# Cosine attention and a highway layer on one Trainium2 core: v's loads on GpSimd's queue, quadrant scores, more turning on TensorE, a new order

## The chip, the cores and the metric

The kernel runs on one core of a Trainium2 chip (trn2). The metric is the time of one execution on the device in microseconds (us). A core has five engines with queues of their own: TensorE (PE: matmuls, and PEld for its weight loads), VectorE (DVE), ScalarE (ACT), GpSimd (POOL) and SyncE (SP). Each works through its instructions in the order in which the program lists them. SP and POOL also issue the transfers (DMAs) here, which 16 DMA engines carry out.

## The reference

```python
def _attn_ref(q, k, v, tau):                   # 8 batches, 12 heads, 448 rows, 64 columns, fp32
    q_n = q / (np.linalg.norm(q, axis=-1, keepdims=True) + 1e-06)
    k_n = k / (np.linalg.norm(k, axis=-1, keepdims=True) + 1e-06)
    scores = np.matmul(q_n, k_n.transpose(0, 1, 3, 2)) / tau
    scores = scores - np.max(scores, axis=-1, keepdims=True)
    attn = np.exp(scores)
    attn = attn / (np.sum(attn, axis=-1, keepdims=True) + 1e-09)
    return np.matmul(attn, v).astype(np.float32)

def _moe_ref(x, w_h, w_t, b_t):                # x: 3584 tokens, 768 columns
    H = np.maximum(x @ w_h, 0.0)
    T = 1.0 / (1.0 + np.exp(-(x @ w_t + b_t)))
    return (T * H + (1.0 - T) * x).astype(np.float32)
```

`reference` runs the attention, puts the heads of a token side by side (`x` is batch and row by head and column), and runs the highway layer on that.

## The kernel before

**Tiling.** Two heads, one of each half of the twelve, form a pair; there are 48 pairs, six to a batch. The 448 rows of a head lie as three columns of 128 partitions and a rest of 64 rows, and the rests of two heads share a column. A finished batch gives three tiles of 128 tokens for the highway layer (`xb`), and the rests of two batches give one more (`xl`): 28 tiles.

**A pair, step by step.** For each batch, q and k are loaded into `raw` (L477, L480 and, for the rests, L494) and turned from fp32 into fp16 on the way. VectorE squares them (`sq`, L532; ScalarE may do it in batch 0, L530), adds up in three steps (L539, L546, L551) and takes the inverse root by a polynomial of six small instructions (L560 to L565, `rs`). A pair's q and k are then scaled into `qkn` (L589, two instructions, on GpSimd, or on VectorE for the first twelve pairs) and turned into `qkT`. For the first six pairs TensorE turns them (L602, seven matmuls with the identity `ident`) and ScalarE or VectorE copies the result out of PSUM (L611, L613); for the others it is a DMA transpose that SP issues (L618). Then come the scores in four steps `qk..._0` to `qk..._3`. Steps 0 to 2 are two matmuls each, in two row halves of the array with 128 columns (L656); step 3 is two matmuls in two 64x64 quadrants (L658). ScalarE takes the exponential of each step (L672, L674). `av` multiplies by v and by a column of ones (L695, 32 matmuls), and `un` divides by the sum (L703, L705, L709).

**v.** A batch of v comes into `vraw` (fp32, L503, 1152 KB, issued by SP) and is cast into `vp` by ScalarE or VectorE (`vc`, L633 or L635); the rests of v go straight into `vp` (`x`, L510, issued by GpSimd).

**The highway layer.** A tile of `xb` is turned by a DMA transpose that SP issues (L747) into `xT`. Four groups `ff` follow (two weights by two halves): six matmuls each (L760), and a seventh for the bias with `w_t` (L763). VectorE takes `d` (L771), ScalarE the tanh (L779), and VectorE ends every second tile in four instructions on PSUM (`e` and `o`, L793, L799), the others in `g` (L809), `h` (L814) and a sum on GpSimd or VectorE (`o`, L822). SP stores (`st`, L836, L839).

**The order.** No loop sets the order. Every piece of work is an `Op` with engines that may do it and their costs, what it depends on, the buffers it takes and gives back (`Ring`), and a step. `Planner.plan` runs a clock over these costs and each time gives a free engine the ready op with the lowest step; it holds DMA queues as `Queues`, in which two transfers side by side pay `MIX`. The steps come from the list `RANKS`, one number for each op. Loads of later batches also wait for the first score step of a pair, and which pair it is stands in the list `HOLDS` (`gates`). What the plan gives is the fixed order of each engine's queue. `NPE = 6` says how many pairs TensorE turns.

Of the kernel before, what the change touches and what calls it, by code (L numbers as in the profile page):

```python
# [20 lines left out]
    -4726, -5034, -3968, -6443, -5016, -1052, -269, -2602, -2552, -2596, -434, 2262, -9024, -8900, -8904, -8800, -8800, -8800,  # L21
    -7024, -8476, -5024, -5024, -4900, -5336, -2524, -2524, -2400, -2398, -2300, -2300, -2300, -2300, 2560, 2976, 3100, 3100,
    3200, 3200, 3200, 3200, 8681, 8922, 9100, 9100, 9200, 9200, 9200, 9200, 14976, 14976, 15100, 15100, 16488, 14761, 15200,
    15200, 20976, 19572, 21100, 21100, 20761, 20761, 21200, 21079, 28179, 28033, 26810, 27100, 25473, 27597, 28022, 27647, 33521,
    33521, 33100, 32877, 33597, 33597, 36754, 33124, -3725, -5674, -5574, 664, 326, 521, 8327, 6326, 6426, 14275, 12373, 11899,
    20275, 20754, 20440, 26230, 25378, 25478, 30637, 32457, 31478, 38275, 36326, 35718, -4873, -5000, -5521, -3528, -4000, -4000,
    -4521, -2528, -2000, -2000, -2521, 2513, -4653, -3653, -1653, 1000, 1000, 1000, 2472, 4000, 3346, 4835, 5472, 1347, 4347,
    6147, 6066, 8213, 8472, 9562, 11213, 11213, 11472, 7347, 13986, 12988, 12500, 14411, 16000, 15546, 12862, 17472, 13347, 17921,
    19000, 19642, 20472, 20589, 22261, 22642, 23472, 18217, 27536, 24941, 24941, 26626, 30536, 27941, 28000, 29472, 25446, 31000,
    31000, 33461, 33230, 34000, 34000, 36173, 35472, 31347, 36112, 36911, 38291, 38472, 40000, 40871, 40000, 38094, 37278, -3500,  # L30
    -3874, -2735, 3134, -2500, -2500, -5046, -40, -1500, -1500, -735, 555, -500, -1324, -799, 499, 500, 500, 1949, -664, 1500,
    3454, 6101, 3555, 2500, 2500, 5167, 3500, 3500, 3645, 3309, 4287, 5258, 5500, 6285, 7156, 7091, 3248, 7258, 7530, 7530, 8529,
    8530, 8500, 10860, 9500, 9079, 11410, 9209, 9209, 12299, 10177, 6379, 13652, 11209, 11209, 15313, 12209, 12209, 16506, 13209,
    13209, 17101, 14209, 14209, 20025, 15209, 15209, 18354, 21987, 17500, 19354, 18500, 18500, 19500, 19500, 18257, 20500, 20500,
    20500, 21500, 21500, 21500, 22500, 22500, 22234, 18725, 23500, 23500, 24204, 26263, 26263, 25534, 27263, 27263, 26500, 28263,
    28263, 27500, 28907, 29263, 28500, 30263, 30263, 31742, 31263, 31263, 30500, 32263, 31630, 31402, 31429, 31500, 32500, 32394,
    32662, 33500, 31201, 33500, 34672, 35218, 34500, 35329, 35486, 35486, 36500, 36818, 36818, 35559, 37500, 37380, 38443, 38380,
    38380, 39500, 38956, 39734, 40500, 40592, 40592, 45215, 41500, 42120, 42322, 42500, 42500, 43322, 44100, 43500, 44322, -675,
    -1000, 5940, 5940, 4026, 9101, 11990, 8050, 9260, 9260, 11841, 15131, 17188, 19871, 20000, 20000, 23000, 24559, 26000, 25079,
    28962, 28451, 32000, 32000, 35000, 35000, 38811, 38811, 41779, 41811, 44000, 44000, 0, 255, 483, 255, 0, 255, 320, 255, 780,  # L40
    900, -1531, 1255, 1000, 1255, 727, 1255, 1000, 1255, 1800, 1891, 696, 2255, 1952, 2255, 2000, 2255, 2000, 2255, 2097, 3767,
    3000, 3136, 3000, 7706, 3000, 2030, 3000, 3136, 3659, 4767, 4000, 3726, 4000, 4255, 4000, 6338, 4000, 4255, 4001, 5767, 4445,
    5255, 5000, 3824, 5000, -3485, 5000, 5255, 5800, 6805, 6000, 7308, 6000, 6255, 6000, 6255, 5623, 6188, 6800, 7272, 7000, 7255,
    7000, 7255, 7000, 7255, 7000, 7255, 7800, 8557, 8000, 8255, 8000, 8230, 8000, 8255, 8000, 8255, 9063, 9767, 9000, 8318, 9000,
    8318, 7689, 8318, 8696, 8318, 9066, 10767, 10000, 12149, 8424, 12808, 10000, 12149, 10000, 12149, 11336, 12489, 11000, 11255,
    10957, 12031, 11000, 11255, 11000, 11255, 11800, 13138, 11857, 12255, 12000, 11895, 12000, 12255, 12000, 12255, 12800, 13767,
    13000, 13255, 13098, 13255, 13000, 14172, 13208, 13255, 16128, 14283, 14000, 14666, 14000, 14255, 14000, 14255, 14715, 14255,
    14800, 14907, 15846, 12782, 15000, 12905, 15622, 12782, 15000, 12782, 15370, 15659, 15208, 15348, 16000, 16255, 16000, 16255,
    16000, 16255, 16800, 17695, 17000, 17805, 17000, 17255, 17000, 17255, 16652, 17255, 17800, 18695, 18000, 18255, 17947, 17991,
    18000, 18255, 18000, 18255, 18800, 19695, 20515, 19255, 20515, 19255, 20515, 19255, 18122, 19255, 20058, 20695, 20000, 20065,  # L50
    20000, 20255, 20000, 20255, 20000, 20255, 19820, 20117, 21083, 21255, 21083, 21255, 21989, 21255, 21393, 21255, 21800, 22695,
    22054, 22255, 21859, 22255, 22237, 23729, 22083, 23465, 22800, 18604, 23083, 24465, 22185, 24465, 23083, 24419, 23078, 24836,
    23822, 27342, 24083, 25318, 24083, 25360, 25764, 25465, 24083, 25465, 24970, 24900, 24921, 26403, 25083, 26468, 25073, 25143,
    24840, 25255, 25800, 26779, 26083, 25996, 24842, 29084, 26083, 25996, 26083, 25996, 26855, 26900, 27083, 26371, 27083, 27017,
    27083, 27017, 27083, 27017, 27800, 27640, 28083, 28224, 28083, 28224, 28083, 28224, 28083, 28224, 27293, 28900, 29083, 29255,
    28137, 29255, 29083, 29255, 28445, 29719, 26915, 29900, 30313, 30255, 30083, 30255, 30000, 30255, 29946, 30428, 27715, 30900,
    31000, 31103, 30423, 31255, 31000, 30253, 31000, 31255, 31567, 31900, 32000, 31568, 32000, 28459, 32000, 28459, 32000, 28459,
    34051, 32900, 31338, 32865, 33000, 33255, 33000, 31864, 33624, 33199, 33567, 33900, 34000, 34255, 34000, 28710, 34000, 28566,
    34668, 28257, 34668, 34900, 35000, 29566, 34843, 29566, 35000, 29566, 35000, 30566, 34777, 35900, 35990, 36255, 36000, 36255,
    36000, 36255, 35741, 33192, 36338, 36900, 37000, 36694, 37000, 37255, 37000, 37255, 37000, 37255, 37567, 37900, 38000, 38475,  # L60
    38241, 38505, 38000, 38475, 38000, 38475, 36529, 39084, 39000, 39255, 39000, 39255, 39000, 40759, 31104, 38789, 40104, 39900,
    40000, 40095, 40000, 40255, 40000, 40255, 40000, 40255, 40567, 43475, 41000, 41255, 41000, 41255, 39907, 41255, 41000, 41255,
    41567, 41900, 42000, 42255, 42000, 42255, 42000, 42255, 42000, 42255, 42800, 42900, 43000, 43255, 41657, 43255, 43000, 43255,
    43000, 43587, 43800, 43900, 44772, 44255, 44261, 44255, 44000, 44456, 44000, 44255, 43771, 45094, 45000, 40783, 44549, 40783,
    45000, 40534, 45000, 40783, 45800, 40862, 46000, 60154, 46000, 45825, 46000, 46472, 44492, 46255, 46800, 39268, 47000, 47108,
    47000, 47255, 47000, 47255, 47000, 47255, 47800, 46158, 3336, 12000, 16736, 23769, 30000, 36634, 42236, 49318, 7317, 9872,
    6036, 9961, 6174, 13150, 319, 8481, 319, 7800, 7800, 7900, 8000, 9317, 11661, 7874, 11914, 8174, 12043, 1692, 12561, 1822,
    4825, 8778, 3458, 8778, 10000, 11317, 13661, 9874, 13961, 9798, 14261, 6557, 14561, 4319, 11800, 6292, 11900, 12000, 13317,
    15661, 9487, 15961, 10483, 16261, 6319, 16561, 6319, 13818, 12577, 13477, 12800, 14000, 14846, 17805, 13474, 17561, 13774,
    17861, 8264, 18161, 7919, 15533, 15147, 15140, 15600, 16390, 18861, 15074, 19161, 15374, 19461, 9519, 19761, 10220, 16817,  # L70
    16689, 16817, 16689, 17200, 14751, 20332, 16674, 20942, 16974, 21783, 12265, 21361, 15417, 18600, 18286, 18700, 18528, 18136,
    16739, 17874, 21961, 18174, 22261, 15472, 22561, 15472, 18352, 18800, 17392, 18800, 19849, 20136, 23661, 19850, 24131, 19737,
# [38 lines left out]
class Ring:  # L111


    def __init__(self, bufs):
        self.free = list(range(len(bufs)))
        self.bufs = bufs
        self.where = {}

    def __getitem__(self, key):
        return self.bufs[self.where[key]]  # L120


class Queues:

# [220 lines left out]
def swdge():  # L345
    return {"POOL": (800, 800, 0.0, False)}
# [558 lines left out]
```

## Time and profile before

| | |
|---|---|
| three runs | 308.23, 304.39, 301.03 us; median 304.39 |
| the profiled execution | 306.19 us, of which the span in the profile is 304.4 us; mean granted clock of TensorE 0.961 |
| PE busy | 245.1 us (81%), 2690 matmuls |
| DVE busy | 226.5 us (74%) |
| ACT busy | 186.3 us (61%) |
| POOL busy | 144.9 us (48%) |
| DMA | q1 (SP's) 57.5%, q0 (POOL's) 44.3% of 16 engines' span |

"Busy" is the time in which at least one instruction of the engine was running. Matmuls overlap each other and their ends are modelled, so the step from one start to the next says more than their length. The span runs from the first to the last instruction; the execution's own time is 1.8 us more.

### The profile page before, as it was taken

The numbers are of one execution on the slowest core, as the hardware profiler recorded it, in microseconds if no ns is written. First come the engines' busy times: TensorE is split into PE (matmuls) and PEld (weight loads), VectorE is DVE, ScalarE is ACT, GpSimd is POOL, SyncE is SP. The second block draws the span as 40 slices with busy tenths as digits, with TensorE's granted clock in tenths as the row PEclk, the third lists the DMA queues.
The fourth block names the chain that finished last, engine by engine and source line by source line (L and its number), as shares of the span: only waits on it lengthen the run. The fifth ranks groups of instructions, "written<-read, shape, count | busy, mean of one in ns | idle before, by whom it ended". The sixth has DMA issues, their size and how long they took to land.

```text
span 304.4 us, 6908 instructions
## 1 busy us (share of the span) xinstructions
PE 245.1 (81%) x2690; PEld 143.0 (47%) x2690; DVE 226.5 (74%) x471; ACT 186.3 (61%) x277; POOL 144.9 (48%) x182
## 2 busy tenths in 40 slices
PE   0032884499498689997999969999699998999992
PEld 0012543155254446553655646465345565556661
DVE  2339689986569976998669896998969865545563
ACT  0273897378557277686659766885178998661221
POOL 8881452036636289337935575547550491002202
PEclk9999999599989999999999998999989999999997
DMA  8999998899969899999999998999999199324523
GB/s 179 118 193 198 177 241 85 145 146 228 141 117 221 137 277 156 213 168 240 228 209 182 178 146 197 135 263 235 187 216 173 65 156 142 71 53 120 155 106 103
DMA packets 125156, 50.99 MB, mean 168 GB/s; under 512 B 106690, under 2 KB 121538, under 8 KB 125123
## 3 DMA queue, kind: packets, MB, share of 16 engines
q1 hardware_dynamic: 79170, 36.39, 57.5%
q0 software_dynamic: 45952, 14.16, 44.3%
q8 instruction: 21, 0.34, 0.4%
q14 instruction: 13, 0.10, 0.1%
HBM read 37.75 MB, written 11.01 MB: 160 GB/s over the span
## 4 chain that ended last, share of the span: by engine, by line
PE 52%; DVE 19%; DMA 15%; ACT 5%; issue 5%; POOL 1%; SPq 1%; DVEq 0%; ACTq 0%; POOLq 0%
PE pb L760 29%; PE pb L695 11%; PE sc L656 7%; DMA vraw<-in_v_dram 7%; ACT ex L672 3%; PE sl L658 3%; DMA w_h<-in_moe_w_h_dram 2%; DMA raw<-in_k_dram 2%; PE pb L763 2%; DMA qkT<-qkn 2%; DVE xb L705 2%; DVE t L809 1%; DVE n L551 1%; DVE sq L532 1%; DVE qkn L589 1%
## 5 line engine op out<-in xcount | busy, mean ns | idle before, releaser
L672 ACT ACTIVATE ex<-sc 128x896 f16<-128x896 f32 x144 | 125.9, 929 | 29.4 <-PE sc L656 29.2
L760 PEld LDWEIGHTS <-xT 128*128 128x128 f16 x672 | 61.8, 99 | 63.3 <-issue 28.9
L589 POOL TENSOR_TENSOR qkn<-raw,rs 128x448 f16<-128x448 f16 x74 | 70.0, 976 | 34.0 <-issue 18.9
L760 PE MATMUL pb<-w_t,xT 128*128 128x384 f16 x336 | 67.3, 339 | 7.5 <-DVE o L799 4.4
L760 PE MATMUL pb<-w_h,xT 128*128 128x384 f16 x336 | 63.8, 331 | 3.2 <-DVE o L799 3.2
L695 PE MATMUL pb<-vp,ex 128*128 128x65 f16 x1536 | 58.4, 195 | 5.9 <-ACT vp L633 3.1
L695 PEld LDWEIGHTS <-ex 128*128 128x128 f16 x1536 | 55.2, 99 | 15.5 <-issue 11.4
L656 PE MATMUL sc<-qkT 64*128 64x448 f16 x288 | 47.0, 370 | 15.3 <-DMA qkT<-qkn 7.2
L771 DVE SCALAR_TENSOR_TENSOR d<-pb,xb 128x384 f16<-128x384 f32 x48 | 26.5, 553 | 11.5 <-PE pb L760 11.1
L779 ACT ACTIVATE pb<-pb 128x384 f32<-128x384 f32 x28 | 13.5, 484 | 28.6 <-PE pb L763 28.3
L779 ACT ACTIVATE t<-pb 128x384 f16<-128x384 f32 x28 | 14.0, 502 | 26.2 <-PE pb L763 26.2
L656 PEld LDWEIGHTS <-qkT 64*128 64x128 f16 x288 | 11.9, 95 | 36.7 <-issue 24.3
L532 DVE TENSOR_TENSOR sq<-raw 128x2688 f16<-128x2688 f16 x15 | 25.2, 1689 | 4.4 <-DMA raw<-in_q_dram 2.4
L705 DVE TENSOR_TENSOR xb<-pb,rd 128x384 f16<-128x384 f32 x48 | 26.8, 558 | 1.7
L822 POOL TENSOR_TENSOR o<-d,xb 128x768 f32<-128x768 f16 x4 | 6.6, 1639 | 45.0 <-DVE d L814 45.0
L510 POOL DMA_DIRECT2D vp<-in_v_dram x16 | 10.9, 682 | 34.5 <-PE sc L656 33.3
L674 ACT ACTIVATE ex<-sl 128x448 f16<-128x448 f32 x48 | 26.9, 561 | 0.4 <-PE sl L658 0.3
L793 DVE SCALAR_TENSOR_TENSOR pb<-pb,d 128x384 f32<-128x384 f32 x28 | 15.6, 562 | 11.6 <-ACT pb L779 11.4
L602 PE MATMUL pb<-ident,qkn 128*128 128x128 f16 x42 | 4.9, 290 | 21.4 <-DVE qkn L589 21.2
L539 DVE TENSOR_TENSOR f<-sq 128x1344 f16<-128x1344 f16 (+2 forms) x17 | 13.8, 810 | 11.0 <-ACT sq L530 10.9
L480 POOL DMA_DIRECT2D raw<-in_k_dram x16 | 13.3, 837 | 14.6 <-PE sc L656 14.4
L763 PE MATMUL pb<-brow,ones 128*128 128x384 f16 x56 | 18.9, 337 | 0.0
(53 smaller groups left out, 239.8 us busy)
## 6 DMA issues: line engine op xcount, KB each, us to landing
vraw<-in_v_dram SPq DMA_DIRECT2D x8, 1152.0 KB, 8.0
out_dram<-o SPq DMA_DIRECT2D x24, 384.0 KB, 2.7
raw<-in_k_dram POOLq DMA_DIRECT2D x14, 288.0 KB, 8.1
raw<-in_q_dram POOLq DMA_DIRECT2D x14, 288.0 KB, 9.0
out_dram<-o SPq DMA_DIRECT2D x8, 192.0 KB, 3.0
w_h<-in_moe_w_h_dram POOLq DMA_DIRECT2D x2, 576.0 KB, 7.1
w_t<-in_moe_w_t_dram POOLq DMA_DIRECT2D x2, 576.0 KB, 10.2
raw<-in_k_dram POOLq DMA_DIRECT2D x16, 48.0 KB, 7.2
```

Source lines behind the costliest of these rows:

```text
L532: nc.vector.tensor_mul(o, r, r)
L589: eng.tensor_mul(qkn_r[n][:, :, g, :], raw_r[b][:, 42 * g + 7 * hn : 42 * g + 7 * hn + 7], rs_r[b][:, g, h].unsqueeze(2).to_broadcast([128 ...
L656: last = nc.tensor.matmul(sc_r[n, j][:, g, 0:S], lhsT=T[:, 128 * j : 128 * j + 128], rhs=rhs, start=True, stop=True)
L672: nc.scalar.activation(o, sc_r[n, j][:, :, 0:S], AF.Exp, scale=inv_tau / (NSC * NSC))
L674: nc.scalar.activation(ex[:, 3136 : 3136 + S], sl_r[n][:, 0:S], AF.Exp, scale=inv_tau / (NSC * NSC))
L695: nc.tensor.matmul(u[:, s * 65 : s * 65 + 65], lhsT=l, rhs=r, start=(m == 0), stop=(m == len(ms) - 1))
L705: nc.vector.tensor_tensor(out=xo, in0=u[:, 0:6, 0:D].rearrange("p (g i) e -> p g i e", g=2), in1=rd[:, 0:6].rearrange("p (g i) -> p g i", ...
L760: nc.tensor.matmul(pt[:, 0:MH], lhsT=xT[:, c, :], rhs=w_sb[w][:, c, ms], start=(c == 0), stop=(w == 0 and c == CC - 1))
L763: nc.tensor.matmul(pt[:, 0:MH], lhsT=ones[:, :], rhs=brow[:, ms], start=False, stop=True)
L771: nc.vector.scalar_tensor_tensor(out=d_r[m][:, h], in0=pb_r[m, w, h][:, 0:MH], scalar=0.0, in1=xsrc()[:, ms], op0=ALU.max, op1=ALU.subtract)
L779: nc.scalar.activation(src if flat else t_r[m][:, h], src, AF.Tanh, scale=0.5)
L793: nc.vector.scalar_tensor_tensor(out=t, in0=t, scalar=1.0, in1=d_r[m][:, h], op0=ALU.add, op1=ALU.mult)
```

## The change

v's loads are issued by GpSimd in place of SP, and the order that `vl[0]` had behind the first load of `raw` is dropped. The score steps 0 to 2 become four matmuls of 64 columns in the four 64x64 quadrants in place of two of 128 columns; step 3 stays as it was. TensorE turns the first twelve pairs (`TPE`, six before) and the first three tiles of x (`XPE`, none before; the copy out of PSUM is done by ScalarE or VectorE). ScalarE may do the squares of batches 0 and 1 (batch 0 before). A first exponential on a small tile (`warm`) stands at the head of ScalarE's queue. Buffers are given back after the last of all their users (`users`), in place of after one named op. Some costs in the planner differ, and `RANKS` and `HOLDS` are new numbers throughout, so the order on every engine is new.

```diff
-    MIX = 12
+    MIX = 4
...
+            for ring, key in op.drops:
+                ring.users[key] = ring.users.get(key, 0) + 1
...
             for ring, key in op.drops:
-                pend.append((op.end + self.SYNC, ring, ring.where[key]))
+                ring.users[key] -= 1
+                if ring.users[key] == 0:
+                    pend.append((op.end + self.SYNC, ring, ring.where[key]))
...
 def swdge():
-    return {"POOL": (800, 800, 0.0, False)}
+    return {"POOL": (730, 730, 0.0, False)}
...
+    def init_act(op):
+        nc.vector.memset(warm[:, :], 0.0)
+        nc.scalar.activation(warm[:, :], warm[:, :], AF.Exp)
+
+    add("warm", {"ACT": (1500, 1500, 0.0, False)}, -30, init_act)
...
         def v_fn(op, b=b):
-            return nc.sync.dma_start(vraw_r[b][:, :, :, :].rearrange("p h c d -> p h (c d)"), heads[2][b])
+            return nc.gpsimd.dma_start(vraw_r[b][:, :, :, :].rearrange("p h c d -> p h (c d)"), heads[2][b])
 
-        vl[b] = add(f"v{b}", sp(650), 6 * b - 4, v_fn, takes=[(vraw_r, b)], dma=("load", 96, 36, 1300, 600))
+        vl[b] = add(f"v{b}", swdge(), 6 * b - 4, v_fn, takes=[(vraw_r, b)], dma=("load", 96, 36, 2200, 800))
...
-            sq = add(f"sq{b}_{lo}", {**dve(n * 64, 2, True), **(act(n * 64) if b == 0 else {})}, s0, sq_fn, deps=ld[b, lo] + ld[b, hi - 1], takes=[(sq_r, key)])
+            sq = add(f"sq{b}_{lo}", {**dve(n * 64, 2, True), **(act(n * 64) if b < 2 else {})}, s0, sq_fn, deps=ld[b, lo] + ld[b, hi - 1], takes=[(sq_r, key)])
...
-    NPE = 6
+    TPE = set(range(12))
...
-        if n < NPE:
+        if n in TPE:
...
                     if j < 3:
-                        last = nc.tensor.matmul(sc_r[n, j][:, g, 0:S], lhsT=T[:, 128 * j : 128 * j + 128], rhs=rhs, start=True, stop=True)
+                        for i in range(2):
+                            o = slice(64 * i, 64 * i + 64)
+                            last = nc.tensor.matmul(sc_r[n, j][o, g, 0:S], lhsT=T[:, 128 * j + 64 * i : 128 * j + 64 * i + 64],
+                                                    rhs=rhs, start=True, stop=True)
...
+        if m in XPE:
+            def xp_fn(op, m=m, xsrc=xsrc):
+                ps = pb_r["x", m][:, 0 : 64 * CC].bitcast(FP16)
+                for c in range(CC):
+                    nc.tensor.transpose(ps[:, 128 * c : 128 * c + 128], xsrc()[:, 128 * c : 128 * c + 128], ident[:, :])
...
-    vl[0].after.append(ld[0, 0][-1])
```

What the new lists make of the head of three queues (the number behind a name is that of the batch for `l`, `r`, `x`, `v`, `sq` and `vc`, and of the pair for the rest; `l` loads q or k, `r` their rests, `x` the rests of v, `w` a quarter of the weights, `iex` clears an `ex` buffer, `nm` is the scaling, `cp` the copy of a turned pair):

```
POOL before: l0 r0 l0 r0 r0 r0 l0 l0 iex x0 x0 l0 iex l0 l0 l0 w ident w iex w l1 l1 l1 l1 r1 r1 nm5 r1 r1 w x1 l2 x1
POOL after:  l0 r0 l0 ident r0 r0 r0 l0 iex l0 l0 l0 l0 l0 iex v0 iex x0 x0 l1 l1 l1 nm1 l1 r1 r1 r1 r1 w w nm3 w nm4 v1 x1
ACT before:  sq0 cp0 ex0 ex0 ex0 ex0 sq0 vc0 vc0 vc0 vc0 cp1 cp2 ex1 ex1 cp4
ACT after:   warm sq0 cp0 sq0 ex0 ex0 ex0 vc0 vc0 ex0 vc0 vc0 cp1 ex1 ex1 ex1 ex1 cp5 sq1 cp3 ex2
SP before:   bias v0 v1 sh0 tr6 tr7 xt0 tr8 tr9 tr10 xt1 tr11 xt2 v2 tr12
SP after:    bias sh0 tr12 st1 tr13 xt3 tr14
```

(`tr` and `xt` are the DMA transposes of a pair and of a tile, `sh` the moves of the rests' output, `st` the stores.) On GpSimd's queue v2 stands behind six of batch 3's eight loads and in front of the scaling of pair 12. On TensorE the order of pairs is no longer one after the other everywhere: pair 29 comes before 26, 40 before 37, 46 before 42.

## The prediction

> **What bounds the kernel now.** I read the page's busy times and chain first, then a table of busy times by stage, then the timeline, and from the starts of the matmuls in it the gaps of TensorE.
>
> ```profile
> PE 245.1 (81%) x2690; PEld 143.0 (47%) x2690; DVE 226.5 (74%) x471; ACT 186.3 (61%) x277; POOL 144.9 (48%) x182
> ...
> PE 52%; DVE 19%; DMA 15%; ACT 5%; issue 5%; POOL 1%; SPq 1%; DVEq 0%; ACTq 0%; POOLq 0%
> ```
> ```profile
> 0.00:15.90 15.90, 0.02 (x1) 0.02 (x2) 5.48 (x23) 2.23 (x2) 13.83 (x30) 1.00 1.09 150
> 15.90:57.30 41.40, 22.02 (x286) 14.04 (x287) 32.63 (x77) 27.06 (x38) 17.15 (x25) 0.94 1.23 175
> 57.30:66.30 9.00, 8.31 (x94) 4.16 (x93) 8.01 (x13) 6.85 (x9) 2.21 (x4) 0.73 0.96 157
> 66.30:110.00 43.70, 34.78 (x383) 19.39 (x382) 34.20 (x70) 25.90 (x39) 22.54 (x26) 0.96 1.12 171
> 110.00:170.00 60.00, 57.51 (x642) 33.22 (x640) 48.72 (x98) 44.10 (x68) 38.08 (x46) 1.00 1.26 210
> 170.00:225.00 55.00, 49.79 (x545) 29.16 (x542) 47.08 (x85) 33.89 (x53) 31.03 (x37) 0.94 1.22 191
> 225.00:298.50 73.50, 72.63 (x756) 42.98 (x754) 48.81 (x108) 45.89 (x72) 20.11 (x19) 1.00 0.56 117
> ```
>
> The columns are stage, length, then PE, PEld, DVE, ACT and POOL busy. TensorE is the bound once it runs; it starts at 15.9 us, limps to 57, and is not full from 66 to 110 and from 170 to 225. I took each gap between two matmul starts, less the pitch of that shape where nothing waits (198 ns for 448 columns, 162 for 384, 31 for 65) and less 95 ns where the array's mode changes. What is over 0.15 us sums to 48.0 us: 22.0 to 57.3 us, 2.5 to 66.3, 11.3 to 110, 2.8 to 170, 8.4 to 225, 1.0 after. So 304.4 = 15.9 start + 234.5 work + 48.0 stalls + 6.0 tail. What stands behind the stalls:
>
> ```profile
> 1.25 6.84 DMA raw<-in_k_dram
> ...
> 65.92 13.72 DMA vraw<-in_v_dram
> 79.66 1.41 DVE vp L635 x2
> ```
> ```profile
> q1 hardware_dynamic: 1554, 1.18, 54.4%
> q0 software_dynamic: 1002, 0.25, 31.4%
> ```
> ```profile
> 175.47 5.50 DVE L814 TENSOR_TENSOR d<-t,d 128x768 f16<-128x768 f16 x1
> 175.93 0.55 ACT L674 ACTIVATE ex<-sl 128x448 f16<-128x448 f32 x1
> 176.05 4.51 POOL L589 TENSOR_TENSOR qkn<-raw,rs 128x448 f16<-128x448 f16 x5
> ```
>
> The first is from the chain of waits: the first k takes 6.8 us to land, and v2 13.7 us, while VectorE stands before its cast. The second is the DMA view of the first 8 us (packets, MB, share): SP's queue has moved all of v0 (1.18 MB) while q and k, issued at the same time, have 0.25 MB. The third is the timeline: `h`, median 0.56 us, takes 5.5 while GpSimd scales pairs back to back. TensorE then stands for PSUM that VectorE has to free (3.1 us at 179; at 215 the same with `g`, 4.2).
>
> **What the Trainium skill says.** "DMA: Bandwidth & Descriptors", Issuing engines are not separate DMA queues: transfers of all engines interleave on the same 16 DMA engines. The trace agrees only in part: beside v0 GpSimd's queue hardly moved. "SBUF — State Buffer", Who interferes with whom: a VectorE instruction with two SBUF inputs blocks against a GpSimd one that reads SBUF. The `h` above agrees. "TensorEngine Tiling (Array Packing)", Key Properties and Restrictions: changing the tiling mode drains the array, and column tiling turns fast weight load off. The trace agrees on the first (a change adds 81 to 108 ns to the pitch); for the second, a quadrant's weight load takes 103 ns against 93. "TensorE: Matmul & The Clock Gate", Step-by-step: weights are pulled ahead of running matmuls. For 64x128 the trace has that (the second step's weights 12 ns after the first step's matmul began); quadrant steps never follow one another in it.
>
> **The change part by part, against the profiled execution's span.**
>
> *Start.* v0 no longer runs beside q and k. The sixth load, the last that the first square needs, was issued at 5.0 and landed at 9.9; `ident` (0.65 us) now stands ahead of it, so 5.65. Loads of the same size (`vp`, L510) land after 2.7 us at best, 3.9 in the median; I take 3.2: 8.9. The table load (1.28 us, shown below) now lies under that wait. The square starts at 8.9 in place of 11.27, and the first turning, 4.6 us on, at 13.5 in place of 15.9.
>
> ```profile
> 9.97 1.28 ACT L530 ACT_TABLE_LOAD   x1 [9.97 <-DMA raw<-in_q_dram]
> ...
> 21.23 1.72 ACT L530 ACTIVATE sq<-raw 128x1792 f16<-128x1792 f16 x1
> ```
>
> *Second pair.* ScalarE ends `cp0` at 15.4, then squares the large part (128x2688: 1.72 x 1.5, an estimate of 2.6) to 18.0, three `ex` at 0.93, one at 0.56 and two `vc` at 0.68 before `ex0_3` to 22.7. v0 is issued near 12.5 behind fewer bytes and lands near 18.5, in time. `av0` (1.0), and `pt1` at about 23.5. VectorE's part for pair 1 (square 1.1, sums 1.6, inverse root 1.3, scaling 0.6) ends near 21, hidden. Before, `pt1` started at 30.8.
>
> *ScalarE's ramp.* Until the first batch is done TensorE has no highway work and ScalarE sets the pace. From `cp1` at 24.4 to the end of `ex7`: seven pairs at 3.35 (3 x 0.93 + 0.56), three `cp` at 0.91, a square 2.6, three `vc` 2.1: 30.8, and 1 for gaps: 56.2. In the old order `ex7` ended near 65. It had a hole of 6.6 us of TensorE from 50 to 56.6, where pair 6 waited for VectorE and for the first DMA transposes (2.9 to 11.6 us, median 3.6); pairs 6 to 11 have none now. Their 42 turnings and the tiles' 18, at up to 107 ns, are 6.4 us of TensorE inside this ScalarE-bound stage; without that cover they would cost it. Copies: 4 more on VectorE, 2 on ScalarE, in the sum. From 57.5 TensorE runs on. At 66 it has ended `qk10_2`, `av7` and all four groups of tile 0; before, at 67.1, `qk8_3`, `av7` and two groups. The lead is 1.1 + seven score steps (1.4) + two groups (2.3) + changes 0.3: 5.1 us.
>
> *After 66 us: v.* Of 23.5 us stalls, 5.9 are v2's (78 to 85), 5.4 VectorE's backlog behind it (to 110), 2.0 v4's (landed 10.3 us after issue), 0.5 v6's: 13.8. On GpSimd's queue a v has its own turn: about 3.2 us of moving (1.18 MB at the 370 GB/s or so of that DMA view's best slices) and 3.2 of latency, 6.5 with no backlog. v2 is issued behind `qk9_0`; its first cast is some 10 us of TensorE work later. v7 is tightest, 8 us. I keep 3 of 13.8. GpSimd pays eight issues at 0.84 to 1.2 us and eight more scalings at 0.94: 16 us more of 145 busy, beside other work.
>
> *Blocked VectorE.* 82 scalings on GpSimd, 74 before; both orders have long runs of them. VectorE loses eight scalings, two squares and six casts and gains five copies: 9 us less. I keep these 7.3 us, and 2.4 of small ones. New: x6 takes `vp` only after `av35`, and `av36` follows 5 us later against 0.7 + 3.9: 1.0. Stalls after 66: 13.7, that is 9.8 less.
>
> *Mode changes.* Counted in the order of TensorE: 217 before, 172 after; after the point above 181 and 141. Before 181 x 0.095 = 17.2; after, into quadrants 94 and out of them 108 ns, 141 x 0.101 = 14.3: 2.9 less.
>
> *Quadrants.* All four share the stream of 448 columns, so no gain; +0 if weights are pulled ahead, +0.1 us a step if not. I take 4 ns for 117 later steps: 0.5.
>
> Sum: 304.4 - 5.1 - 9.8 - 2.9 + 0.5 = 287.1 us of span, 288.9 as an execution. The profiled one was 306.19 against a median of 304.39; in that measure 287.2, rounded to 287.5.
>
> **Rivals.** (a) The later stalls stay (VectorE held by GpSimd, loads late elsewhere): 287.1 + 9.8 = 297 span, 297 as a median, 2.4% faster. For: the fixed orders bet on durations, and transposes vary from 2.9 to 11.6 us. Against: v's lateness is named in the chain. (b) Quadrant weights are not pulled ahead: 117 x 0.1 = 11.7, 299, within 2%. (c) Better: the v stalls go entirely, VectorE's relief takes half of the blocked time, and 13.7 falls to 6: 279.5. (d) Slower: GpSimd's queue sets the pace at each batch turn. Pair 12's scaling stands behind v2 and two loads that wait for `qk11_0`: 0.68 + 0.84 + 1.87, then a transpose of 3.6, 7.0 us, against 8.8 of TensorE work up to `qk12_0`: 1.8 slack. If v's packets lengthen that by 6.3, six turns lose 4.5 each: 27, 314. It passes before's time at 2.8 us a turn and +2% at 3.8.
>
> **How the numbers follow.** Forecast 0.50, (a) 0.20, (b) 0.08, (c) 0.13, (d) 0.09. A change of about 2% is what a measurement of this kernel can tell from none. Faster: 0.50 + 0.13 + 0.14 of (a) = 0.77; same: 0.06 of (a) and (b) 0.08 = 0.14; slower 0.09. Range 275 to 302: (c) less 4.5 and (b) with 3 on top, which is the doubt about the lead at 66 us; (d) is outside.
>
> **What would show it.** Right: first turning at 13 to 14 us, `pt1` before 25, no PE hole at 50 to 57, v landing in 6 to 8 us with no cast waiting over 1 us, 448-column steps 200 ns apart. Wrong: steps 300 ns apart; GpSimd's loads waiting while `qk` waits for `qkT`; VectorE's `g`, `h` and squares stretched by more than 20 us in sum.

## The result, and the profile after

The changed kernel takes 316.64 us (median of four runs, 316.22 to 317.75), the kernel before, run beside it, 302.85: ratio 1.048 [1.040, 1.057] (the brackets are a 95% interval). It is slower. A ratio, here and below, compares the undisturbed executions of the two kernels alone, so it need not be the quotient of their medians. The profiled span is 314.5 us, at a granted clock of 0.962 against 0.961.

From the page, busy times and chain of the changed kernel:

```profile
PE 251.8 (80%) x3038; PEld 150.0 (48%) x3038; DVE 222.2 (71%) x460; ACT 196.8 (63%) x289; POOL 165.6 (53%) x200
...
PE 44%; DMA 18%; DVE 16%; POOL 10%; issue 5%; ACT 3%; SPq 2%; DVEq 0%; POOLq 0%; ACTq 0%
PE pb L804 26%; DMA qkT<-qkn 9%; PE pb L720 8%; DMA xT<-xb 6%; PE sc L680 6%; POOL qkn L609 5%; DVE sq L551 3%; DMA raw<-in_q_dram 2%; DVE qkn L609 2%; PE pb L807 2%; POOL raw L513 2%; POOL raw L499 2%; DVE f L558 1%; DVE n L570 1%; DVE o L866 1%
```

GpSimd has grown by 21 us and VectorE has shrunk by 4, but what is new is the second line's POOL, and what its DMA is made of. v's load is in the chain no longer; in its place stand the two kinds of DMA transposes (`qkT<-qkn`, `xT<-xb`). The table by stage (length, then PE, PEld, DVE, ACT, POOL busy, granted clock, DMA share, GB/s) shows where:

```profile
12.90:57.30 44.40, 30.30 (x427) 20.20 (x428) 35.22 (x77) 35.90 (x46) 28.75 (x38) 1.00 1.14 172
57.30:66.30 9.00, 8.81 (x110) 5.26 (x110) 7.34 (x12) 8.74 (x13) 6.39 (x10) 1.00 1.64 178
66.30:110.00 43.70, 36.24 (x456) 20.85 (x451) 32.55 (x69) 28.45 (x44) 22.71 (x28) 0.92 1.06 167
110.00:170.00 60.00, 48.23 (x596) 28.04 (x594) 38.19 (x78) 37.62 (x56) 38.96 (x43) 0.94 1.14 185
170.00:225.00 55.00, 47.07 (x524) 27.12 (x524) 41.94 (x77) 29.84 (x45) 27.65 (x32) 0.94 0.95 148
```

Up to 66.3 us TensorE does more than before (it starts at 12.9). From 110 to 170 us it now idles 11.8 us, against 2.5. Stalls counted as in the prediction: 40.0 us after 66.3 us, against 23.5 before and 13.7 forecast. Put into the prediction's sum, 287.1 + 26.3 = 313.4, that is nearly all of the miss. (Of the 40.0, 29 are in the view of waits and some 5 are steps at half speed after long stands, for which see the last section.) What TensorE waited for most after 66 us, changed kernel first, then the kernel before (line that waits <- releaser: us in all, times, longest):

```profile
PE sc L680 <- DMA qkT<-qkn: 12.9, 6, 5.7
PE pb L804 <- DMA xT<-xb: 7.1, 3, 5.0
PE pb L804 <- DVE d L815: 2.5, 1, 2.5
PE sc L680 <- ACT ex L697: 2.0, 6, 0.5
PE pb L720 <- DVE o L843: 1.9, 1, 1.9
```
```profile
PE pb L760 <- DVE o L799: 7.6, 4, 4.4
PE sc L656 <- ACT ex L672: 3.6, 3, 1.9
PE pb L760 <- DVE d L771: 2.1, 1, 2.1
...
PE sc L656 <- DMA qkT<-qkn: 0.7, 2, 0.6
```

Before, TensorE waited for VectorE. After, it waits 20.0 us for transposes, in nine waits. The longest, from the timeline and the chain of the changed kernel (start, length, what):

```profile
73.87 1.07 POOL L522 DMA_DIRECT2D vraw<-in_v_dram  x1
```
```profile
73.94 9.56 DMA qkT<-qkn
```
```profile
75.65 2.20 PE L720 MATMUL pb<-vp,ex 128*128 128x65 f16 x64
83.55 0.96 PE L680 MATMUL sc<-qkT 64*64 64x448 f16 x8 [5.69 <-DMA qkT<-qkn]
```

v3 and pair 12's transpose are issued in the same 0.1 us, from two queues. The transpose lands after 9.6 us and TensorE stands for it. The DMA view from 76 to 80 us (packets, MB, share) says what the DMA engines did meanwhile:

```profile
q0 software_dynamic: 188, 0.87, 78.2%
q1 hardware_dynamic: 462, 0.12, 20.0%
```

GpSimd's queue moves 0.87 MB, SP's 0.12. The same view from 75 to 77.1 us, and then from 77.1 to 79.5, shows that it isn't a slow trickle:

```profile
q1 hardware_dynamic: 896, 0.23, 83.5%
q0 software_dynamic: 15, 0.07, 9.0%
```
```profile
q0 software_dynamic: 145, 0.67, 100.6%
```

By 77.1 us the transpose's whole 0.23 MB (128x896 in fp16) has moved. After that SP's queue moves nothing for 2.4 us, though a store and a second transpose have been issued on it. A transfer has landed when its semaphore has had sixteen updates; those of the transpose come in the trace between 80.6 and 83.5 us, each about 0.2 us ahead of one of v3's. So it ends when v3 ends, 6.4 us after its last data packet began. Why its end stands behind v3, the trace doesn't tell. The first 8 us of the kernel before are the same with the roles exchanged: v0 on SP's queue moved first, and GpSimd's queue moved nothing until 5.5 us, though its first load was issued at 1.25. It is not always so: where both queues move, they go packet for packet (631 against 628 in the kernel before from 74 to 77 us), and the longer packets take the more bytes.

Over the 54 transposes with a landing in the trace: with nothing of GpSimd's queue in flight at their issue the median is 2.8 us (24 of them, the longest 5.5), with 400 KB or more, of v or of q and k, it is 8.5 us (18 of them, from 2.7 to 10.3).

### The profile page after: what moved, and what is told of

Same layout as the page of the kernel before. It is cut to its first block, busy times and chain, and to the rows that moved or that the text cites. A ratio compares the mean times of both kernels' runs of the same rounds, so it can differ in the third digit from the quotient of the medians.

```text
span 314.5 us, 7570 instructions
## 1 busy us (share of the span) xinstructions
PE 251.8 (80%) x3038; PEld 150.0 (48%) x3038; DVE 222.2 (71%) x460; ACT 196.8 (63%) x289; POOL 165.6 (53%) x200
## 4 chain that ended last, share of the span: by engine, by line
PE 44%; DMA 18%; DVE 16%; POOL 10%; issue 5%; ACT 3%; SPq 2%; DVEq 0%; POOLq 0%; ACTq 0%
PE pb L804 26%; DMA qkT<-qkn 9%; PE pb L720 8%; DMA xT<-xb 6%; PE sc L680 6%; POOL qkn L609 5%; DVE sq L551 3%; DMA raw<-in_q_dram 2%; DVE qkn L609 2%; PE pb L807 2%; POOL raw L513 2%; POOL raw L499 2%; DVE f L558 1%; DVE n L570 1%; DVE o L866 1%
## 5 line engine op out<-in xcount | busy, mean ns | idle before, releaser
L804 PEld LDWEIGHTS <-xT 128*128 128x128 f16 x672 | 63.2, 100 | 67.5 <-issue 25.4
L609 POOL TENSOR_TENSOR qkn<-raw,rs 128x448 f16<-128x448 f16 x82 | 79.3, 990 | 20.4 <-DVE rs L584 13.2
L680 PE MATMUL sc<-qkT 64*64 64x448 f16 x576 | 52.9, 392 | 25.9 <-DMA qkT<-qkn 12.9
L804 PE MATMUL pb<-w_h,xT 128*128 128x384 f16 x336 | 65.3, 339 | 8.4 <-DMA xT<-xb 7.1
L815 DVE SCALAR_TENSOR_TENSOR d<-pb,xb 128x384 f16<-128x384 f32 x48 | 26.5, 554 | 26.5 <-PE pb L804 25.5
L680 PEld LDWEIGHTS <-qkT 64*64 64x64 f16 x576 | 16.5, 108 | 50.3 <-issue 29.8
L866 POOL TENSOR_TENSOR o<-d,xb 128x768 f32<-128x768 f16 x6 | 9.8, 1641 | 57.5 <-DVE d L858 54.8
L823 ACT ACTIVATE t<-pb 128x384 f16<-128x384 f32 x28 | 13.7, 496 | 27.1 <-PE pb L807 26.8
L529 POOL DMA_DIRECT2D vp<-in_v_dram x16 | 10.9, 693 | 32.7 <-PE sc L680 18.2
L551 DVE TENSOR_TENSOR sq<-raw 128x2688 f16<-128x2688 f16 (+1 forms) x14 | 23.0, 1640 | 5.8 <-DMA raw<-in_q_dram 4.5
L837 DVE SCALAR_TENSOR_TENSOR pb<-pb,d 128x384 f32<-128x384 f32 x28 | 15.8, 563 | 12.7 <-ACT pb L823 12.5
L728 DVE RECIPROCAL rd<-pb 128x7 f32<-128x7 f32 x48 | 9.6, 199 | 18.2 <-PE pb L720 17.9
L624 PE MATMUL pb<-ident,qkn 128*128 128x128 f16 x84 | 8.8, 266 | 14.2 <-DVE qkn L609 14.2
L683 PE MATMUL sl<-qkT 64*64 64x448 f16 x96 | 18.5, 372 | 0.6 <-ACT ex L699 0.5
```

What stands on the lines that cost most here:

```text
L551: nc.vector.tensor_mul(o, r, r)
L609: eng.tensor_mul(qkn_r[n][:, :, g, :], raw_r[b][:, 42 * g + 7 * hn : 42 * g + 7 * hn + 7], rs_r[b][:, g, h].unsqueeze(2).to_broadcast([128 ...
L680: last = nc.tensor.matmul(sc_r[n, j][o, g, 0:S], lhsT=T[:, 128 * j + 64 * i : 128 * j + 64 * i + 64], rhs=rhs, start=True, stop=True)
L683: nc.tensor.matmul(sl_r[n][r, 0:S], lhsT=T[:, 832:896] if g == 0 else T[:, 384:448], rhs=rhs, start=True, stop=True)
L804: nc.tensor.matmul(pt[:, 0:MH], lhsT=xT[:, c, :], rhs=w_sb[w][:, c, ms], start=(c == 0), stop=(w == 0 and c == CC - 1))
L815: nc.vector.scalar_tensor_tensor(out=d_r[m][:, h], in0=pb_r[m, w, h][:, 0:MH], scalar=0.0, in1=xsrc()[:, ms], op0=ALU.max, op1=ALU.subtract)
```

## The experiments

Stalls are those of TensorE after 66.3 us, in us; the last two columns are the sums of its waits for DMA transposes and for VectorE in the view of waits. All three come from one profiled execution of each kernel. Kernels that leave work out are marked *. A ratio is to the kernel before as run in the same group; for two kernels none could be formed. The kernels were run in seven groups, and the kernel before had medians from 300.9 to 304.5 us in them, single executions from 295.2 to 312.1. So ratios of different groups are not to be set against each other, and a difference of some 3 us between the medians of two groups settles nothing.

| kernel | median us | ratio to before | stalls | DMA | VectorE |
|---|---|---|---|---|---|
| before | 302.85 | 1 | 23.5 | 0.7 | 12.7 |
| changed | 316.64 | 1.048 [1.040, 1.057] | 40.0 | 20.0 | 6.5 |
| e2_v_twelfth* | 302.86 | 1.018 [1.000, 1.037] | 26.5 | 9.1 | 7.3 |
| e3_v_fp16 | 314.43 | 1.062 [1.048, 1.077] | 36.6 | 17.9 | 7.4 |
| e4_before_v_pool | 305.70 | 1.031 [1.021, 1.042] | 23.9 | 11.0 | 4.3 |
| e8_loads_later | 313.33 | 1.057 [1.040, 1.073] | 36.3 | 17.3 | 7.4 |
| e6_v_actq | 315.78 | 1.031 [1.015, 1.047] | 31.2 | 15.1 | 6.0 |
| e7_halves | 321.33 | 1.050 [1.033, 1.066] | 34.5 | 18.3 | 5.2 |
| e10_v_pieces | 310.42 | 1.027 [1.015, 1.039] | 31.3 | 11.8 | 7.4 |
| e9_light* | 306.03 | 1.013 [1.006, 1.020] | 29.4 | 4.6 | 14.4 |
| e11_before_quads | 307.85 | 1.021 [1.012, 1.030] | 30.8 | 0.3 | 14.1 |
| e12_before_quads_v0 | 304.01 | none | 22.3 | 1.4 | 6.3 |
| e13_light_scal* | 285.54 | 0.951 [0.943, 0.960] | 10.9 | 4.5 | 0.5 |
| e14_breath | 322.07 | 1.064 [1.056, 1.073] | 44.6 | 23.0 | 6.2 |
| e15_handshake | 307.39 | 1.012 [1.002, 1.021] | 29.0 | 15.8 | 2.7 |
| e16_both | 307.30 | 1.022 [1.004, 1.039] | 36.8 | 15.7 | 2.8 |
| e17_both_loads | 301.72 | 1.012 [1.000, 1.025] | 25.9 | 11.0 | 0.6 |
| e18_before_handshake | 299.78 | none | 13.4 | 1.9 | 3.2 |
| e19_best | 295.94 | 0.984 [0.976, 0.991] | 11.7 | 0.8 | 1.7 |

The first theory (T1): v on GpSimd's queue keeps the transposes from landing. Its rival (T2): the new order puts work right behind transposes that also run beside loads of q and k. In the code cuts `...` marks what is left out.

**Less of v.** Changed kernel; from batch 2 on one head of v of twelve is loaded.

```diff
-            return nc.gpsimd.dma_start(vraw_r[b][:, :, :, :]..., heads[2][b])
+            h = slice(0, NH if b < 2 else 1)
+            return nc.gpsimd.dma_start(vraw_r[b][:, h, :, :]..., heads[2][b][:, h])
```

> The changed kernel, its order untouched; from batch 2 on v's load brings one head of twelve (the other heads of v are left as they were two batches before). Theory T1 (v's load on GpSimd's queue moves in packets of 4608 bytes and keeps DMA transposes from moving beside it; TensorE waits for the turned pairs): the stalls at pairs 12, 21 and 24 go, some 13 us; 316.6 becomes 302 to 305, and transposes issued beside v land in about 3 to 4 us in place of 7 to 10. Theory T2 (the new order puts work right behind transposes that run beside q's and k's loads, whatever v does): 313 or more, and the stall of 5 us before the first group of tile 10 stays. The two can add: then 302 to 305 with that stall still there.

13.8 us less than the changed kernel, as T1 has it, and the stalls fall by 13.5. But 26.5 us of stalls are left, twice the prediction's 13.7, and three waits for transposes of x are still 6.5 us, beside loads of q and k as before. So both theories hold, and T1 is one half only.

**v as fp16.** v is cast on the way (`vraw` FP16). In the trace its packets then have 384 bytes, against 4608 in the changed kernel and 768 from SP's queue before.

> The changed kernel, its order untouched; v is turned into fp16 on the way in, as q and k are, so its packets are 384 bytes instead of 4608 and the buffer vraw is fp16. All of v is still moved on GpSimd's queue. T1 in its narrow form (the size of the packets does it): transposes share with v one packet for one, land beside v in 5 to 6 us in place of 7 to 10; 304 to 310. T1 in its wide form (any v load on that queue does it, because it takes 3 to 5 us of the DMA engines): 313 to 317. T2: 313 to 317.

314.4 (312.6 to 317.2), so little or nothing is gained. In the view of waits TensorE stands for the transposes as in the changed kernel, though v has half the bytes in SBUF and a twelfth of the packet:

```profile
PE sc L680 <- DMA qkT<-qkn: 11.3, 6, 5.0
PE pb L804 <- DMA xT<-xb: 6.6, 4, 3.5
```

From 77.1 to 79.5 us SP's queue again moves nothing, beside 897 packets of 384 bytes. So the narrow form of T1, that long packets block short ones, falls. The runs fit the wide form, that any load of v does it for as long as it runs.

**The old order with v1 to v7 from GpSimd's queue.**

> The kernel before, its order untouched; v of batches 1 to 7 is issued by GpSimd at the same place of the order, v of batch 0 stays with SP. T1: transposes beside v are held up here too (7 to 10 us to landing), but v itself lands 2 to 6 us sooner and VectorE's wait for it shrinks: 300 to 312, with stalls of TensorE on turned pairs that the kernel before has not. T2: no slower than before, 298 to 304, since the old order leaves transposes room.

3.1% slower than the kernel before by the ratio (medians 305.7 and 300.9 in its group), while the stalls of the two traces are alike, 23.9 and 23.5. v's own lateness near 78 us goes (0.7 us of stalls from 60 to 80, 5.4 before), and transposes come late in its place:

```profile
PE pb L761 <- DMA xT<-xb: 7.1, 4, 5.9
PE sc L657 <- DMA qkT<-qkn: 3.9, 3, 2.4
```

The queue alone, without the new order, turns a late v into late transposes and gains nothing on balance.

**v from ScalarE's queue**, in the changed kernel's order (`nc.scalar.dma_start` in place of `nc.gpsimd.dma_start`).

> The changed kernel, but all eight loads of v are issued from ScalarE's DMA queue instead of GpSimd's; the order stays. Theory 1 (a v load that comes from GpSimd's queue keeps SP's transposes from moving; a load from a hardware queue alternates with them packet by packet): transposes beside v land in 3 to 5 us, the gap of TensorE at 78 to 89 us shrinks from 8.6 to under 3, the time falls to 302 to 306 us. Rival (any 1.18 MB that moves beside the transposes takes their time, from whichever queue): tr12, tr21 and tr24 still land in 7 to 10 us and the time stays at 313 to 317.

Pair 12's transpose is issued 2.8 us later than in the changed kernel and lands at 83.1 us, where it landed at 83.5; v3 lands at 82.2. TensorE still waits 15.1 us for transposes in all, and the median is 315.8 (309.6 to 319.9). So it is mostly the rival: from whichever queue v comes, it takes the transposes' time. The Trainium skill says so ("DMA: Bandwidth & Descriptors", Issuing engines are not separate DMA queues: all run on the same 16 engines and interleave); these runs agree that another queue is no separate path, and add that for a few us one queue can stand whole (SP's, 77.1 to 79.5 us of the changed kernel).

**v in pieces behind single transposes**, from SP's queue, four pieces of three heads each, for the three v that collide.

```diff
...
+    for b, behind in ((3, ("tr12", "tr13", "xt3", "tr14")), (4, ("tr21", "xt7", "xt8", "xt9")), (5, ("tr26", "tr24", "tr28", "tr25"))):
+        order.remove(by[f"v{b}"])
+        for p, n in enumerate(behind):
+            by[n].fn = lambda op, fn=by[n].fn, b=b, p=p: (fn(op), piece(b, p))[0]
```

> The changed kernel, but v3, v4 and v5 (those that collide with transposes) go from SP's queue in four pieces of three heads, each issued behind one transpose (tr12, tr13, xt3, tr14; tr21, xt7, xt8, xt9; tr26, tr24, tr28, tr25). Nothing is left out. Theory 1 with its repair: a transpose now waits at most for a piece ahead of it in its own queue, about 1 to 2.5 us; the gaps at 78 to 89, 132 and 158 us fall by 8 to 11 us together and the time to 305 to 309 us. Rival (the bytes themselves are what delays them): 312 to 317.

310.4, 6 us better than the changed kernel and just above what T1 expected; TensorE waits 11.8 us for transposes in place of 20.0, and for a pair's never longer than 1.7. It is a repair of part of the DMA loss, with every byte still loaded.

**Loads of q and k later.** Batch 6's five loads stand behind the first highway group of tile 10, and wait for it.

> The changed kernel; the five loads of batch 6's q and k that begin beside the DMA transposes of tiles 10 to 13 are moved behind the first group of tile 10 and wait for it; all else keeps its order. T2: the stall before that group (5.1 us, and 3.6 us of half clock after it) goes: 307 to 311. T1 alone: 314 to 317, since v is not touched.

3.3 us by the medians, about as much as the groups differ. In the traces the stalls from 160 to 180 us fall from 9.4 to 3.6, those from 180 to 200 rise from 2.2 to 5.9. T2's place is right, but more than half of its gain is given back 20 us later.

**Both kinds of loads cut.** e2, and from batch 3 on one head of three of q and k.

> The changed kernel that loads one head of v of twelve from batch 2 on, and from batch 3 on one head of three of q and k (the big loads only); the rest of those loads is left out. It says how much of the loss after 66 us is DMA traffic of all kinds beside the transposes. If all of the transposes' lateness is (v and q/k together): stalls of TensorE after 66 us fall to 10 to 14 us, as predicted, and the time to 289 to 294 us. If the order itself puts work too close behind transposes, or VectorE and GpSimd hold each other up: 298 to 303, near the 302.9 of the kernel that drops v alone.

306.0 us: most of the traffic is gone, and the time is no better than e2's 302.9. Waits of TensorE after 66 us:

```profile
PE pb L807 <- DVE d L818: 5.1, 3, 3.4
PE pb L723 <- DVE st L737: 4.6, 3, 3.5
PE pb L807 <- DMA xT<-xb: 3.0, 2, 1.7
PE pb L723 <- DVE d L818: 2.6, 1, 2.6
...
PE pb L723 <- DVE o L846: 2.1, 1, 2.1
PE sc L683 <- DMA qkT<-qkn: 1.6, 1, 1.6
```

With transposes nearly on time (4.6 us of waits) those for VectorE come up, 14.4 us in place of 6.5. Behind them is one picture, here in the timeline of the changed kernel:

```profile
113.30 4.50 POOL L609 TENSOR_TENSOR qkn<-raw,rs 128x448 f16<-128x448 f16 x5
...
114.56 4.07 DVE L866 TENSOR_TENSOR o<-d,xb 128x768 f32<-128x768 f16 x1
...
119.14 1.32 PE L804 MATMUL pb<-w_t,xT 128*128 128x384 f16 x6 [2.50 <-DVE d L815]
```

`o`, 0.95 us at its shortest on VectorE, takes 4.07: it begins as the second of the five scalings runs and ends 0.8 us after the last. `d`, which frees PSUM for TensorE, stands behind it.

**GpSimd's scalings cut as well.** e9, and for pairs 12 to 47 3 of 7 columns of chunks are scaled.

> e9_light (the changed kernel without most of v from batch 2 and of q and k from batch 3) with GpSimd's scalings of pairs 12 to 47 over 3 of 7 columns of chunks; the rest of them is left out too. It asks what holds the 29 us of stalls after 66 us that e9_light still has. Theory B (VectorE, held by GpSimd's runs of scalings, with the half-speed matmuls that follow a long stall): VectorE's waits before TensorE fall from 14 to under 5 us, stalls after 66 us to 12 to 17, time to 291 to 296 us. Rival (the order's own waits on ScalarE and on transposes): less than 4 us faster than e9_light's 306.

285.5 us, 20.5 less than e9 and below the forecast for the whole. What is left of waits for VectorE:

```profile
PE pb L808 <- DVE o L847: 0.3, 1, 0.3
PE pb L724 <- DVE st L738: 0.2, 1, 0.2
```

Stalls after 66.3 us are 10.9, less than the forecast 13.7. So the two causes together are large enough for the whole miss. Taken away alone, v's traffic still leaves 26.5 us and all big loads 29.4, since VectorE's waits come up behind the transposes'. This run takes work from GpSimd too, so by itself it doesn't tell blocked from overloaded. The next two do.

**A break between scalings**: a write of 128x1 zeros on GpSimd.

> The changed kernel, and between two of GpSimd's scalings (from pair 12 on) that directly follow one another stands a write of 128x1 zeros to a spare tile on GpSimd. Nothing is left out. Theory B1 (VectorE's two-input work is kept out because the scalings leave no break between them): VectorE's stretched instructions fall from 18.7 us to under 8, TensorE's waits for VectorE to under 3 us, the time by 5 to 9 us to 308 to 312. Rival B2 (a short write makes no break, only the amount of GpSimd's reading counts): no change, 315 to 319.

Slower by 5 us. I count an instruction of VectorE as stretched when it takes over 0.5 us more than the shortest of its line and shape (the expectation's 18.7 us was counted in another way). The excess goes from 20.6 to 18.5 us only, that of gates, products and sums from 12.1 to 9.6. The writes add 3.8 us to GpSimd's busy time, and TensorE waits longer for transposes (23.0 us). So a short write between the scalings hardly lets VectorE in.

**A handshake**: the first scaling that follows a gate or sum of VectorE (`g`, `h`, `o`) in the written order waits until that has ended.

```diff
...
+            if op.eng == "DVE" and op.ins is not None and op.name[0] in "gho":
+                port = op
+            if op.eng == "POOL" and op.name.startswith("nm") and port is not None and port.ins is not None:
+                tc.add_manual_dep(op.ins.ins, port.ins.ins.name, info, reason="a scaling begins behind VectorE's last two-input work")
+                port = None
```

> The changed kernel, with a wait added on GpSimd: the first scaling that stands behind a gate product or an output sum of VectorE in the written order begins only when that has ended. Nothing is left out. Theory B1: the long stretches (o 2.5 us, h 3.0, g 2.1 in excess) go, since at most one scaling is under way when VectorE's instruction starts; 4 to 7 us faster, 310 to 313. Rival B3 (GpSimd is then late: its scalings feed transposes that TensorE waits for already): the time stays within 2 us of 316.6 or grows, and tr waits grow by what VectorE's shrink.

307.4 us (305.1 to 310.1), 9 less than the changed kernel and better than expected, with all work in place. The same `o` in its timeline:

```profile
113.41 0.95 DVE L866 TENSOR_TENSOR o<-d,xb 128x768 f32<-128x768 f16 x1
```
```profile
114.44 3.62 POOL L609 TENSOR_TENSOR qkn<-raw,rs 128x448 f16<-128x448 f16 x4 [1.55 <-DVE o L866]
```

GpSimd stands 1.55 us, then runs its scalings in a row; `o` takes 0.95 in place of 4.07. No gate, product or sum is stretched by 0.5 us any more (20.6 us of excess in all fall to 8.5; squares, first sums and VectorE's own scalings of the ramp remain). GpSimd has as much work as before, so what stretched VectorE was the blocking and not the load. The transposes land as late as ever beside big loads (8.2 us in the median). TensorE's waits for VectorE fall by 3.8 us and those for transposes by 4.2, its steps at half speed by about 3: the gain isn't VectorE's alone.

**Both repairs.** e15 and e10 together (e16_both), and that with e8's later loads (e17_both_loads).

> The changed kernel with both repairs, nothing left out: v3, v4 and v5 in four pieces each from SP's queue behind single transposes (as in e10_v_pieces), and the handshake of e15_handshake (a scaling of GpSimd waits for VectorE's gate product or output sum ahead of it). If DMA and VectorE are two separate losses, the gains add: 316.6 - 6.2 - 9.2 = 301 us, range 298 to 304, just below the kernel before. Rival (each repair only moved TensorE up to the other's wait): 305 to 308, no better than e15_handshake.

307.3 us (302.0 to 313.3), ratio 1.022 [1.004, 1.039]: no better than the handshake alone in the median, 3 us better in its best execution (302.0 against 305.1). Its row in the table is from its slowest execution. Whether the gains add isn't settled by it.

> e16_both, and batch 6's five loads of q and k behind the first highway group of tile 10, as in e8_loads_later. There it gave 3.3 us. If it is given back again by pair 36's late transposes: within 1.5 us of e16_both; otherwise 2 to 4 us faster, 297 to 300.

301.7 us, ratio 1.012 [1.000, 1.025], 5.6 below e16: here the later loads are not given back. All three repairs bring the changed kernel to about the kernel before, not below it. TensorE still waits 11.0 us for transposes in it, and 8.4 for ScalarE, 4.3 of these in one wait that ends at 138 us.

**The quadrants.** The changed kernel with halves of 64x128 again:

> The changed kernel with its score steps as two halves of 64x128 again, as before the change; everything else and the order stay. The prediction priced the quadrants at +0.5 us for themselves, and 2.9 us of gain for fewer changes of mode between quadrant scores and the quadrant left-over scores. If that holds, this kernel is 2 to 4 us slower than the changed one where TensorE is the bound, less where it stands for transposes: ratio to the changed kernel 1.00 to 1.01. If the quadrants cost something that the trace doesn't show, it is faster by more than 3 us.

The median is 4.7 us above the changed kernel's, in another group and with a wide spread (315.1 to 327.4), so the times don't settle it. In the trace TensorE's work (last start less first start less stalls) is 242.1 us, against 236.0, and mode changes are 231 against 172: 59 at 95 ns are 5.6. So the quadrants save TensorE work in this order, mostly in changes of mode; in this execution of the halves smaller stalls (34.5 us against 40.0) hide it. And alone in the old order:

> The kernel before with one part of the change alone: its score steps in four 64x64 quadrants; the order stays the old one. The trace of e7_halves has 242.1 us of TensorE work (last start less first start less stalls), that of the changed kernel 236.0: 6.1 us for the quadrants together with the changes of mode that they save, where the prediction had 2.4. Theory Q (the quadrants are worth 4 to 6 us by themselves): work falls from 234.2 to 228 to 230 us and the time by 3 to 6 us, ratio 0.980 to 0.990. Rival 1 (the gain is given back in later waits, since VectorE and the transposes set the pace): the stalls grow by as much and the ratio is 0.995 to 1.005. Rival 2 (quadrants cost more than halves, and e7_halves was slow for another reason): above 1.01.

Work falls by 2.2 us, near the prediction's 2.4 (55 changes fewer at 95 ns would be 5.2 by themselves, so an estimate of 3 is lost again), but the kernel is 2.1% slower by the ratio. In its profiled execution, one of its slowest (312.2 us), stalls rise by 7.3; ScalarE stands longer for v4 (2.3 us before):

```profile
147.30 0.67 ACT L633 CAST vp<-vraw 128x576 f16<-128x576 f32 x1 [6.01 <-DMA vraw<-in_v_dram]
```

The ratio lies in rival 2's range, above 1.01, but TensorE's work fell and didn't grow; so it is rival 1's mechanism, and more than it forecast. That an order written for one pace loses when TensorE's pace changes would explain it, but isn't shown; how much of the 2.1% that one wait is, no run here tells.

**The start**, on top of e11: v0 from GpSimd's queue behind q and k, and the table loaded first.

> e11_before_quads with two more parts of the change, both at the start: v0 from GpSimd's queue behind the loads of q and k (v1 to v7 stay on SP's), and ScalarE's table loaded by a small activation before anything else. The prediction had the first turning 2.4 us earlier, and the changed kernel's trace had it (12.9 against 15.9). If the lead is carried through ScalarE's ramp: 2 to 3 us faster than e11_before_quads. Rival (the old order gives it back by 66 us, since the first DMA transposes and VectorE's part for pair 6 come no earlier): within 1 us of e11_before_quads.

304.0 against e11's 307.9; the first turning comes 0.8 us earlier, not 2.4, probably since the loads' order on GpSimd's queue is the old one. The size agrees with the expectation, the spread (294.7 to 310.3) is too wide to lean on it.

**The old order with the handshake**, and then with the start as well:

> The kernel before with the handshake alone, nothing else of the change. Its VectorE loses 14.5 us to stretched gates and products, and TensorE waits 12.7 us for VectorE after 66 us. If the handshake works there as in e15_handshake: 5 to 9 us faster, ratio 0.970 to 0.985. Rival (the old order leaves GpSimd less room, so that transposes come later): ratio 0.99 to 1.01.

299.8 us against 304.3, though the executions overlap (293.5 to 303.2, and 295.2 to 312.1) and no ratio could be formed. TensorE's waits for VectorE fall from 12.7 to 3.2 us and its stalls after 66.3 us from 23.5 to 13.4; the second is flattered, as the profiled execution is one of the quickest here (296.3) and was not for the kernel before (306.2). The loss to blocked VectorE was there before the change.

> e18_before_handshake (the kernel before with the handshake) plus the change's start: v0 from GpSimd's queue behind the loads of q and k, and ScalarE's table loaded first. The two touch different stretches: e12_before_quads_v0 gained about 3 us on e11_before_quads with this start. If it adds: 296 to 298 us, ratio to the kernel before 0.965 to 0.985, the fastest of all kernels here that leave nothing out. Rival (the old ramp up to 66 us gives it back): within 1 us of the 299.8 of e18_before_handshake.

295.9 us, ratio 0.984 [0.976, 0.991]: some 1.6% faster than the kernel before, and faster than the changed one, with nothing left out; all its six executions (294.0 to 296.0) lie below those of the kernel before in this group (297.5 to 306.5). Of its waits after 66 us:

```profile
PE sc L658 <- ACT ex L674: 5.2, 3, 3.5
PE sc L658 <- DMA qkT<-qkn: 0.8, 3, 0.3
PE pb L762 <- DVE st L711: 0.5, 1, 0.5
```

## Why the prediction was wrong

- *Start, second pair, ramp: right.* First turning at 12.9 (13.5 forecast), `pt1` (the turning of pair 1) at 25.2 (23.5; its sign, before 25, is just missed), `ff0_11` ended at 66.2 and `qk10_2` at 66.8 (66): a lead of about 4.5 us in place of 5.1. At 50 to 57 no gap is longer than 0.9 us.
- *Quadrants and mode changes: right in kind.* Quadrant steps that follow each other start 213 to 214 ns apart, not 200, so the term of 117 steps is about 1.6 us in place of 0.5 (an estimate from these steps); the weights are pulled ahead, or it would be 300. Changes cost 92 to 94 ns in and 83 to 108 out.
- *"After 66 us: v": this step failed.* v's lateness did go: no wait for v's load is in the chain. It lands 8.1 us after issue, not 6.5. But I asked only who waits for v, and not what moves while v moves. The term is the transpose, priced at 3.6 us, its old median; beside a large load it is 8.5. "I keep 3 of 13.8" became 20.0 us of waits for transposes, and with v all but gone (e2) the stalls fall by 13.5 us, half of the 26.3 that the forecast lacked. The table of before had the warning: v0 beside q and k, 1.18 MB against 0.25, was read as a fact of the start. The planner priced it lower still: the change took `MIX`, what it adds for a transfer beside another, from 12 to 4. Whether an order made with 12 would leave transposes more room, no run tells.
- *"Blocked VectorE ... I keep these 7.3": this step failed too.* I read it as a stall of fixed size. It is a second limit behind the first: with transposes nearly on time the waits for VectorE were 14.4 us (e9), and with GpSimd's scalings cut as well the stalls are 10.9 (e13). Had v been harmless, as forecast, the time would still have been near e2's 303, not 287.5: transposes beside q and k (9.1 us of waits in e2) and VectorE (7.3) hold the other half of the miss.
- *Rivals.* (d) had the place and the first price right: pair 12's scaling stands behind v2 and loads, the transpose must fit into a slack of 1.8 us, and the wait there is 5.7. It named GpSimd's queue as what is late, though; here it was the transfer beside it, and only part of its six turns lost. That its 314 met the span of 314.5 is luck, as the sum is a different one. (a) was half right: VectorE held by GpSimd did stay. (b) didn't happen. Of the signs of being wrong, none came as written: `g`, `h` and squares were stretched by 7.7 us, not 20, and no sign asked how long a transpose takes beside v.

## What to carry to other kernels

When a large transfer moves to another queue, list what moves at the same time on every queue and who waits for that: the gain on the transfer may return as lateness of small ones. Where a second wait sits just behind the one that you remove, price both removed together, and ask what remains of each alone. A VectorE instruction stretched beside a run of GpSimd work can be helped: a wait that lets VectorE's instruction end first cost GpSimd seven stands here, of 0.2 to 1.6 us and 5.0 in all, and the kernel was 9 us faster.

## What the runs showed of the hardware

- While a 1152 KB load runs on one queue, a transpose on another lands only as the load ends: its 0.23 MB had moved in 1.9 us, its end came 6.4 us later, and SP's queue moved nothing for 2.4 us. Packets of 384 bytes in place of 4608 don't help (e3), nor does ScalarE's queue in place of GpSimd's (83.1 against 83.5 us, e6).
- A break of one tiny write between GpSimd's scalings hardly lets VectorE's two-input instruction in (18.5 against 20.6 us of excess); a wait does (8.5). "SBUF — State Buffer" of the Trainium skill, Who interferes with whom, names the blocking, and the `o` of 4.07 us agrees; that a wait ends it is e15's.
- A long stand of TensorE can cost more than itself. After the one that ends at 119.1 us five matmuls of 384 columns start 162 ns apart, and the next eight about 320: the granted clock is 1.00 through the stand and 0.51 from 119.9 to 122.9. After 66 us such steps add up to about 5 us in the changed kernel, 3 in the kernel before, 0.2 in e13, where all its waits together are 7.9 us.
